# RWKV-7 recurrence and top-k expert layer on one core: 32 by 32 blocks to and from GpSimd's inversion, by transfers or by VectorE's turns

## The chip, the cores and the metric

The kernel runs on one core of one Trainium2 chip, whose engines are TensorE (PE), VectorE (DVE), ScalarE (ACT), GpSimd (POOL) and SyncE (SP). The metric is device time in microseconds (us) of one execution of the whole kernel, lower is better. Profiles show one execution; its span (first to last instruction) and its own time stand beside the median of the timed runs below.

## What is computed

The first part is a recurrence over 768 tokens for 4 batches of 8 heads with head size 40, each with a 40 by 40 state. The second part routes each of the 3072 output rows (320 wide) to one of 8 experts, keeps the 80 rows with the highest gate weight per expert, and runs them through a two-layer network:

```
for t in range(S):                       # S = 768
    y[t]  = r[t] @ state
    Sa    = state @ a[t]
    state = state * w[t] - outer(Sa, b[t]) + outer(v[t], k[t])

x = y as (3072, 320);  logits = x @ w_gate
expert = argmax(logits);  gate = softmax(logits)[expert]
per expert e: keep the 80 rows of largest gate
out[rows] = gate * (relu(x[rows] @ w1[e]) @ w2[e])   # other rows are zero
```

## The kernel before, in words

**Units.** The sequence is cut into 12 chunks of 64 tokens; the 4 batches go in 2 pairs. A unit is one chunk of one pair, 24 units in all, n = 2 * chunk + pair. In a unit all 8 heads of both batches are handled together; one "block" is the 64 by 64 triangular matrix of one head and batch, 16 blocks in a unit. Within a chunk the recurrence becomes matrix products, with one inverse of a 64 by 64 unit-triangular matrix for each block.

**`prepare(n)`** (L498) loads w, a, k, b, forms the running products of w (two scans on VectorE, L514 and L522), turns and scales, and makes the score matrices: `nt` (the matrix to be inverted) and `psi`. It holds `P`, `ah`, `kb`, `psi` of a unit in rings of LOOK = 9 (L262), so unit n can only be prepared once unit n - 9 is done with them; `nt` has a ring of 8 units, so unit n's scores also need unit n - 8 to be done with its inverse. **`finish(n)`** (L732) loads r and v, uses the inverse (L846, L865), adds up outputs and the new state (L901, L914, L934, L939), and hands the output rows to **`gate`** (L971), once for four units (for two units at the very end). A unit's finish needs the state of the unit two before.

**The inverse.** For the first four units it is made by repeated squaring on TensorE (`doubling`, L419). For units 4 to 23, in five batches of four units, it goes by halves: each 64 by 64 matrix has two 32 by 32 diagonal blocks, 128 of them in a batch, which GpSimd inverts, one block in each of its 128 partitions, by 60 row steps (L648, L650), an `affine_select` and a `memset` (L655). So 32 by 32 blocks that lie across 32 partitions have to be laid flat, one in each partition, and back. `invert` (L601) does this through three tensors in HBM:

- SyncE writes the blocks out (`out_go`, L623, four DMAs) and GpSimd fetches them flat into `lt` (L632); SyncE also clears the lower left corners of `nt` (L640);
- after the steps GpSimd makes a flat transposed copy `ltT` (`flip`, L661) and writes both out (L668);
- SyncE brings them back: `solved` into `d1` (L677, four DMAs) and into `nt` (L684), `flipped` into `d0` (L690).

**`solve(n)`** (L698) joins the halves of a unit: matmuls G (L708) give, with all 128 rows as contraction over block-diagonal operands `d0`, an off-diagonal product that ScalarE copies to `gt` (L713); matmuls X (L723) with `d1` give the corner, which ScalarE copies into `nt` (L728). One join is eight matmuls of 128 rows, 64 columns, 64 wide.

**Ranks.** `gate` keeps for each group of four units the 80 best of 128 new and 80 old gate values in a row: ten rounds of `max` (L1026) and `match_replace` (L1028) over 208 columns on VectorE, five groups (`ranks`, L1022). Then the rows are joined in 8 partitions (L1041 to L1050), and three sets of ten rounds over 320, 336 and 336 columns follow, the last when the last two units have their gates. From their result `best` the selection, the gather and the expert layer follow.

**What sets the order.** All instructions of the first part are given to `Plan` (L18) with a planned duration, a due time and the tiles they read and write. `Plan.order` simulates the engines and writes down one fixed order for each engine (PE, DVE, ACT, POOL, and SP for its DMAs); ring reuse and PSUM banks are dependencies in it. A table `WISH` (L148) shifts due times by kind of operation and stage, `SAME` and `SWITCH` price a change between whole-array and tiled matmuls. On the chip each engine works through its order and waits where a semaphore isn't there yet; an SP DMA that waits holds every later SP DMA. With `held_back` (L739) the loads of r and v of a unit also wait for its batch's blocks to have been written out.

**Second part.** When the first part's buffers are free, the weights of 8 experts (L1095 to L1098) stream in on SP's queue while the selection runs; then 6 passes of gather, two layers and scatter.

Of the kernel before, what the change touches and what calls it, by code (L numbers as in the profile page):

```python
# [17 lines left out]
class Plan:  # L18
# [7 lines left out]
    def add(self, eng, us, lag, when, fn, reads=(), writes=(), psum=None, to=()):  # L26
# [21 lines left out]
        self.ops.append(o)  # L48

# [95 lines left out]
SAME = 88.8  # L145
WHOLE = ("wT", "aT", "ivT", "kbTp", "rvT", "sTp", "xp", "gp", "G", "X")
USE_TAIL = True
WISH = {  # L148
    "ACT UL": (4.2, 0, 19.2), "ACT VL": (-96.9, 27.8, -94.1), "ACT W": (2.1, 0, -24.8),
    "ACT W0": (-34.4, -152.3, -9.7), "ACT d0": (0.7, 20.3, -15), "ACT d1": (-14.1, 5.1, 10.3),  # L150
    "ACT dec": (5.1, 3.5, -35.1), "ACT el": (0, -105.4, -111.1), "ACT gt": (-14.2, 9.3, 21.8),
    "ACT ivc": (0.6, 0, 22.4), "ACT kbT": (46.6, 4.9, 29.8), "ACT nt": (-170.6, -112.1, 3.6),
    "ACT rawa": (11.7, 40.7, -2.7), "ACT rawb": (6.6, 0, -61.5), "ACT rs": (-8.4, 69.6, 4.2),
    "ACT rv": (22, 7.8, 4.1), "ACT sT": (14.3, -12.2, -3.8), "ACT uT": (59.9, -9.9, -23.9),
    "ACT xg": (8.9, 22.7, 4.9), "DVE P": (167.3, -8.9, 23.5), "DVE UL": (9.8, -12.3, -5.5),
    "DVE VL": (-65.4, -31.3, 3.6), "DVE W": (-36.1, -44.8, -5.4), "DVE ah": (73.7, 4.7, -113.1),
    "DVE begins": (14.6, 5.3, 15.4), "DVE cd": (240.3, 350.6, -16.3), "DVE consts": (-2, -35.6, -2.3),
    "DVE d0": (86.6, 16.4, -85.6), "DVE d1": (0, -24.8, 9.6), "DVE dec": (-11, 63.1, 27.1),
    "DVE ends": (-16.2, -79.7, 10), "DVE gates": (-23.5, 11, -44.9), "DVE gsm": (22.7, -33.7, 18.8),
    "DVE iv": (-0.2, 1.7, -5.2), "DVE jn": (10.1, 207.1, 243.7), "DVE kb": (-48, 7.9, -240.3),  # L160
    "DVE late": (-46.4, 1.9, 2.3), "DVE lg": (68.6, -5, -39.1), "DVE lt": (6.9, 26.2, 0),
    "DVE ltT": (-2.7, -53.8, 0.6), "DVE nt": (6.3, 0, -12.2), "DVE psi": (52.4, 66, -77.2),
    "DVE rawa": (4.8, 17.7, -76.6), "DVE raww": (10.4, -32, -11.4), "DVE rs": (0, 8.3, -30),
# [16 lines left out]
}  # L180
RQ = "SP"
VQ = "SP"
ALPHA = 1.9451


@with_exitstack
def kernel(
# [29 lines left out]
    GU = 4  # L217
# [53 lines left out]
    with ExitStack() as p1:  # L271
# [24 lines left out]
        def group(name, n):  # L296
            return wide[name][(n // GU) % WIDE[name]]
# [4 lines left out]
        def bank(key):  # L302
            return plan.home[key]
# [115 lines left out]
        def doubling(n, z, kn):  # L419


            def spare(name):
                return quads_of(name, n)
# [873 lines left out]
```

## Time and profile before

| | |
|---|---|
| median of 3 runs | 583.64 us (580.11 to 585.15) |
| the profiled execution | 579.1 us |
| its span | 577.3 us |
| PE busy | 450.2 us (78%) |
| DVE busy | 342.2 us (59%) |
| ACT busy | 208.8 us (36%) |
| POOL busy | 222.1 us (38%) |
| mean granted TensorE clock | 0.907 |
| last copy of a recurrence output (L964) ends | 465.1 us |
| `best` complete | 479.6 us |
| first expert matmul (L1224) | 501.9 us |

Busy is time in which an engine ran an instruction. The five inversions on GpSimd work from 92.7 to 132.7, 175.2 to 216.9, 237.4 to 277.6, 305.5 to 345.9 and 371.1 to 407.8 us (first step to the memset). In the views, x counts instruction records: each fp32 matmul shows as two, so the eight matmuls of a join are "x16". "idle before" is what the engine stood still before an instruction, and behind the arrow what ended it; "issue" there means that the profile shows nothing that it waited for.

### The profile page before, as it was taken

What the parts mean: (1) busy time and instruction counts of PE and PEld (TensorE: products, weight loads), DVE (VectorE), ACT (ScalarE), POOL (GpSimd) and SP (SyncE); (2) the same over time, 40 slices, a digit from 0 to 9 for tenths busy, and PEclk for the clock granted to TensorE, in tenths of its full rate; (3) what the DMA queues carried; (4) which work ended last, traced back from release to release, by engine and by line L of the source; (5) the groups of instructions that cost most, each with busy time, mean ns of one, the idle gap of its engine ahead of it and who ended that gap; (6) DMA issues with size and microseconds to landing.
All of it is one profiled execution on the core that took longest, in us unless ns stands there. A gap on an engine that the chain in (4) does not pass through costs nothing. (4 is left out here: it accounts for less than half of the span.)

```text
span 577.3 us, 28139 instructions
## 1 busy us (share of the span) xinstructions
PE 450.2 (78%) x12655; PEld 370.3 (64%) x12655; DVE 342.2 (59%) x752; ACT 208.8 (36%) x424; POOL 222.1 (38%) x412
## 2 busy tenths in 40 slices
PE   3878977788688988389976998698759813399996
PEld 2767767778687977289876897588648712134432
DVE  8878863556357865486643675875478897112211
ACT  2435543545434654145524463344414300011010
POOL 7000005882107982588407982388400010400101
PEclk9989998989979998699979998799969965599999
DMA  8745572614987648845789335721530139999200
GB/s 137 120 70 94 95 134 61 102 49 99 262 143 149 99 91 202 168 71 112 158 148 182 59 82 133 156 37 33 139 84 16 26 99 359 348 344 342 86 13 17
DMA packets 243452, 73.91 MB, mean 128 GB/s; under 512 B 216484, under 2 KB 237988, under 8 KB 243332
## 3 DMA queue, kind: packets, MB, share of 16 engines
q1 hardware_dynamic: 218292, 51.15, 43.4%
q10 hardware_dynamic: 22304, 11.29, 7.3%
q0 software_dynamic: 2736, 9.67, 5.0%
q8 instruction: 99, 1.62, 1.2%
q14 instruction: 21, 0.17, 0.1%
HBM read 52.11 MB, written 16.72 MB: 119 GB/s over the span
## 5 line engine op out<-in xcount | busy, mean ns | idle before, releaser
L648 POOL TENSOR_TENSOR tmp<-lt 128x30 f32<-128x30 f32 (+9 forms) x150 | 82.9, 553 | 27.3 <-DMA lt<-blocks 15.9
L650 POOL TENSOR_TENSOR lt<-lt,tmp 128x30 f32<-128x30 f32 (+9 forms) x150 | 85.0, 567 | 11.7
L632 POOL DMA_DIRECT2D lt<-blocks x5 | 3.0, 596 | 142.9 <-PE ps L468 76.9
L575 PE MATMUL ps<-ah,kbT 40*64 40x64 f32 x1536 | 33.8, 223 | 9.8 <-issue 8.0
L575 PEld LDWEIGHTS ps<-ah,kbT 40*64 40x64 f32 x1536 | 28.1, 136 | 11.9 <-issue 7.8
L754 ACT COPY VL<-rawv 128x320 f32<-128x320 f32 x24 | 11.0, 459 | 64.5 <-PE ps L901 55.4
L901 PE MATMUL ps<-UL,kb 64*64 64x128 f32 x768 | 29.9, 291 | 4.8 <-DVE UL L789 3.2
L564 ACT COPY kbT<-ps 128x1024 f32<-128x1024 f32 x24 | 24.4, 1015 | 24.0 <-PE ps L408 21.1
L514 DVE TENSOR_TENSOR_SCAN P<-dec,begins 128x520 f32<-128x520 f32 x24 | 32.1, 1337 | 0.6
L522 DVE TENSOR_TENSOR_SCAN iv<-dec,ends 128x520 f32<-128x520 f32 x24 | 31.8, 1326 | 0.7
L1255 POOL DMA_INDIRECT out_dram<-y,idx_s x6 | 6.0, 997 | 66.8 <-DVE y L1254 66.8
L789 DVE TENSOR_TENSOR UL<-ps,mask 128x512 f32<-128x512 f32 x24 | 16.5, 689 | 25.1 <-PE ps L782 24.9
L901 PE MATMUL ps<-VL,kb 64*64 64x128 f32 x768 | 29.4, 288 | 0.7 <-issue 0.7
L408 PE MATMUL ps<-ident,kb 128*128 128x128 f32 x192 | 27.7, 290 | 2.1 <-DVE kb L547 1.1
L1224 PE MATMUL hp<-w,xe 128*32 128x512 f32 (+1 forms) x128 | 28.4, 643 | 0.7 <-DVE xe L1214 0.7
L1252 PE MATMUL yp<-w,hT 128*64 128x320 f32 (+1 forms) x256 | 28.6, 435 | 0.3 <-DVE hT L1243 0.3
L944 DVE TENSOR_TENSOR xT<-ps,P 128x512 f32<-128x512 f32 x24 | 16.5, 687 | 20.9 <-PE ps L901 20.9
L708 PE MATMUL ps<-d,nt 128*64 128x64 f32 x320 | 16.1, 250 | 15.6 <-issue 8.0
L765 ACT COPY rv<-ps 128x1024 f32<-128x1024 f32 x24 | 24.4, 1015 | 9.7 <-PE ps L408 9.7
L901 PEld LDWEIGHTS ps<-UL,kb 64*64 64x64 f32 x768 | 23.6, 143 | 6.6 <-DVE UL L789 4.0
L914 PE MATMUL ps<-rv,sT 40*64 40x64 f32 x768 | 23.8, 232 | 4.7 <-issue 4.7
L956 PE MATMUL ps<-wsel,xT 128*128 128x88 f32 x192 | 25.8, 279 | 0.8 <-DVE xT L944 0.8
(201 smaller groups left out, 1117.8 us busy)
## 6 DMA issues: line engine op xcount, KB each, us to landing
w<-in_moe_w_dram SPq DMA_DIRECT2D x8, 1280.0 KB, 14.3
w<-in_moe_w_dram SPq DMA_DIRECT2D x8, 1024.0 KB, 15.5
x_rows<-xg ACTq DMA_DIRECT2D x24, 160.5 KB, 3.8
rawk<-in_k_dram SPq DMA_DIRECT2D x48, 80.0 KB, 3.3
raww<-in_w_dram SPq DMA_DIRECT2D x48, 80.0 KB, 3.2
rawr<-in_r_dram SPq DMA_DIRECT2D x48, 80.0 KB, 3.0
rawv<-in_v_dram SPq DMA_DIRECT2D x48, 80.0 KB, 2.9
out_dram<-zero ACTq DMA_DIRECT2D x8, 480.0 KB, 3.3
```

Source lines behind the costliest of these rows:

```text
L408: nc.tensor.matmul(o, lhsT=i, rhs=ident, start=True, stop=True, is_transpose=True, skip_group_check=True)
L514: nc.vector.tensor_tensor_scan(at("P", n), at("dec", n)[:, 0 : H * SEG], begins, 0.0, op0=Alu.mult, op1=Alu.add)
L522: nc.vector.tensor_tensor_scan(at("iv", n)[:, H * SEG : 0 : -1], at("dec", n)[:, H * SEG : 0 : -1], at("ends", n)[:, H * SEG : 0 : -1], 0. ...
L564: nc.scalar.copy(at("kbT", n).rearrange("p (k c) -> p k c", k=2), ps[:, bank(kk) : bank(kk) + 2, :])
L575: nc.tensor.matmul(ps[T * o : T * o + T, b0 + q, T * i : T * i + T], lhsT=at("kbT", n)[rows, 512 * x + c : 512 * x + c + T], rhs=at("ah", ...
L648: e.tensor_tensor(out=tv, in0=t3[:, 0:s, s : s + 1].to_broadcast([np_, s, n]), in1=t3[:, s : s + 1, s + 1 :].to_broadcast([np_, s, n]), op ...
L650: e.tensor_tensor(out=t3[:, 0:s, s + 1 :], in0=t3[:, 0:s, s + 1 :], in1=tv, op=Alu.add)
L765: nc.scalar.copy(at("rv", n).rearrange("p (k c) -> p k c", k=2), ps[:, bank(kr) : bank(kr) + 2, :])
L901: nc.tensor.matmul(ps[HB * q : HB * q + HB, b0 + bb, 128 * i : 128 * i + 128], lhsT=at("kb", n)[rows, o : o + HB], rhs=view(at(name, n)[ro ...
L956: nc.tensor.matmul(ps[:, b0, o : o + 88], lhsT=at("xT", n)[:, 128 * i : 128 * i + 128], rhs=wsel[:, i, :], start=True, stop=True, skip_gro ...
L1224: nc.tensor.matmul(hp[j][c], lhsT=xe[:, i, c], rhs=weights[e][0][:, i, FH * j : FH * j + FH], start=i == 0, stop=False)
L1252: nc.tensor.matmul(yp[c], lhsT=hT[:, f, c], rhs=weights[e][2][:, f, :], start=f == 0, stop=f == FK - 1)
```

## The change

1. **Blocks by turns.** The three HBM tensors and all transfers of `invert` are gone. VectorE's `transpose`, which turns each 32 by 32 square within 32 partitions, moves the blocks: three turns in (one over all 128 partitions with 1024 columns, two over 32 partitions with 1024 columns, strided views), then the same GpSimd steps, then four turns out: `d0` and `tb` (128 partitions each) and two of 32 partitions back into `nt`. The flat copy `flip` and the corner clearing are gone; the copy of the scores into `nt` leaves the corner out (three ScalarE copies in place of one, the corner is zeroed once by GpSimd at the start).
2. **Joins on 32-row tiles.** `d0` and `tb` hold only 32 by 32 blocks. G and X are sixteen matmuls each: 32 rows, 32 or 64 columns, 32 wide, into two PSUM banks (before: one); `gt` and the corner are copied with two ScalarE copies of 32 or 64 partitions each. G and X are no longer listed as whole-array in the planner.
3. **Ten units in flight.** LOOK is 10; `P`, `ah`, `kb`, `psi` of a unit lie in one tile. Slots 8 and 9 serve first as scratch of the doubling in place of the old `d0` and `d1`; half of the doubling's `plus` lies in the new `d0`.
4. **Ranks of 16 units at once.** Groups 0 to 3 lay their 128 values side by side; ten rounds over 512 columns follow at group 3, ten over 208 columns at group 4. The later sets stay.
5. **Planner.** New `WISH`, `ALPHA`, `SAME`; planned durations for the new operations (1.2 us for a turn, 1.53 us for a round over 512). The r and v loads are no longer held back.

```diff
-    blocks, solved, flipped = (nc.dram_tensor(name, (len(batches), 2, 2, 2, GU * H // 2, C * C), F32, kind="Internal")
-                               for name in ("blocks", "solved", "flipped"))
-    LOOK = 9
+    LOOK = 10
...
             if n >= GU:
                 def nt_go():
-                    nc.scalar.copy(quads_of("nt", n), quads(kn).rearrange("p q (i t) -> p q i t", t=T))
+                    o, i = quads_of("nt", n), quads(kn).rearrange("p q (i t) -> p q i t", t=T)
+                    nc.scalar.copy(o[:, :, :, C:], i[:, :, :, C:])
+                    for x in range(2):
+                        rows = slice(T * x, T * x + C)
+                        nc.scalar.copy(o[rows, :, :, 0:C], i[rows, :, :, 0:C])
...
         def invert(kq):
+            def by_s(c):
+                return view(group("nt", ns[0]), C * c, (1, C), (T, C))
+            by_h = view(lt, 0, (1, C), (C, C))
+            for x, c in ((None, 0), (0, 1), (1, 1)):
+                rows = slice(0, 128) if x is None else slice(T * x + C, T * x + T)
+                add("DVE", 1.2, 0.1, z, lambda rows=rows, c=c: nc.vector.transpose(by_h[rows], by_s(c)[rows]),
+                    [("nt", n) for n in ns], [lk])
 ...
-            add("SP" if x == 0 or whole else "ACT", 0.8 * 2 * len(qs), 2.4, z, out_go, [("nt", n) for n in ns], [("blk", kq, x)])
-            add("POOL", 1.0, 4.6, z, fetch, [("blk", kq, 0), ("blk", kq, 1)], [lk])
-            add("SP", 0.7 * 2 * len(qs), 1.9, z, clear_go, (), [("nt", n) for n in ns])
...
-            add("POOL", 2.05, 0.1, z + 4.1, flip, [lk], [("ltT", kq)])
-            add("POOL", 1.0, 3.7, z + 4.2, put("lt", solved), [lk], [("sol", kq)])
-            add("POOL", 1.0, 4.6, z + 4.3, put("ltT", flipped), [("ltT", kq)], [("flp", kq)])
-            add("SP", 2.9, 2.0, z + 5, d1_go, [("sol", kq)], [("d1", n) for n in ns])
-            add("SP", 0.8 * 2 * len(qs), 2.6, z + 5, d0_go, [("flp", kq)], [("d0", n) for n in ns])
-            add("SP", 0.8 * 2 * len(qs), 3.2, z + 5, nt_back_go, [("sol", kq)], [("nt", n) for n in ns])
+            add("DVE", 1.2, 0.1, z + 5, lambda: nc.vector.transpose(view(at("d0", kq), 0, (1, C), (C, C)), lt.rearrange("p (s t) -> p s t", s=C)),
+                [lk], [("d0", kq)])
+            add("DVE", 1.2, 0.1, z + 5, lambda: nc.vector.transpose(view(at("tb", kq), 0, (1, C), (C, C)), by_h), [lk], [("tb", kq)])
+            for x in range(2):
+                rows = slice(T * x, T * x + C)
+                add("DVE", 1.2, 0.1, z + 5, lambda rows=rows: nc.vector.transpose(by_s(0)[rows], by_h[rows]), [lk], [("nt", n) for n in ns])
...
+            def joined_by(key, rows_of, lhs, rhs, outs):
+                b0 = bank(key)
+                for q in range(2):
+                    for i in range(M4):
+                        for x in range(2):
+                            rows = slice(*rows_of(x))
+                            o = C * (M4 * q + i)
+                            nc.tensor.matmul(ps[outs(x), b0 + x, o : o + C], lhsT=lhs(rows, q, i), rhs=rhs[rows, q, i, :],
+                                             start=True, stop=True, skip_group_check=True)
-            held_back = [("blk", batch_of[n], 1)] if n >= GU else ()
...
-                ranks(cd, nx, [("cd", gi), ("cd", gi + 1)], 0.89, False)
+                if lastly:
+                    ranks(later, nx, [("cd", 1), ("cd", 0)], 0.89, False)
+                elif len(groups[gi + 2]) < GU:
+                    ranks(early, later, [("cd", 0), ("cd", 1)], 1.53, False)
```

## The prediction

> **What bounds the kernel now.** I read the busy shares first, then stage sums, then the waits in order of time, and last the costs of single groups. The stage sums come from the table of windows, cut where joins of a batch begin (163, 240, 302, 365, 425 us), at the end of the recurrence (465) and before the expert layer (502). Columns: stretch and length, then busy us of PE, PEld, DVE, ACT, POOL.
>
> ```profile
> 163.00:240.00 77.00, 64.00 (x1834) 57.11 (x1826) 54.27 (x125) 35.24 (x72) 44.62 (x80) 0.92 0.69 138
> 240.00:302.00 62.00, 52.71 (x1608) 48.08 (x1609) 35.41 (x69) 25.65 (x53) 36.99 (x60) 0.89 0.66 125
> 302.00:365.00 63.00, 55.21 (x1733) 49.78 (x1733) 38.22 (x70) 30.73 (x64) 39.92 (x69) 0.97 0.57 114
> 365.00:425.00 60.00, 42.19 (x1394) 38.54 (x1394) 38.69 (x124) 20.50 (x47) 36.49 (x72) 0.86 0.46 99
> 425.00:465.00 40.00, 35.47 (x1187) 31.78 (x1187) 33.46 (x96) 14.09 (x35) 0.39 (x2) 0.95 0.08 16
> 465.00:502.00 37.00, 6.44 (x38) 4.11 (x40) 23.32 (x73) 1.14 (x7) 8.14 (x16) 0.52 0.87 283
> 502.00:577.30 75.30, 69.43 (x511) 29.05 (x511) 13.83 (x23) 7.85 (x20) 5.98 (x6) 0.95 0.52 169
> ```
>
> PE leads everywhere up to 425 us, but it is idle for 13.0, 9.3, 7.8 and 17.8 us there, 47.9 in all. From 417.5 (gates of group 4, timeline) to 479.6 (`best`) VectorE sets the pace: ranks, units 20 to 23 and gates follow one another. The timeline shows what PE stood still for:
>
> ```profile
> 243.50 1.12 PE L708 MATMUL ps<-d,nt 128*64 128x64 f32 x16 [7.60 <-issue]
> 371.35 1.09 PE L723 MATMUL ps<-d,gt 128*64 128x64 f32 x14 [4.83 <-DMA d<-solved]
> 425.29 1.33 PE L708 MATMUL ps<-d,nt 128*64 128x64 f32 x16 [6.86 <-DMA d<-flipped]
> ```
>
> All three are joins that wait for blocks. The first is named "issue", but its `d0` DMA was issued at 239.90, behind one of 8.22 us for `d1`. The steps had been over since 216.9, so the way back took 26.6 us; the last batch took 17.5 (407.8 to 425.3). The way in is 12 to 13 us (225.5 to 237.4, 292.8 to 305.5, 358.0 to 371.1). The steps themselves take 37 to 42 us.
>
> ```profile
> 407.65 0.16 POOL L658 MEMSET lt<- 128x32 f32 x1
> 408.10 0.60 POOL L668 DMA_DIRECT2D solved<-lt  x1 [0.30 <-POOL lt L658]
> 408.71 1.96 POOL L662 COPY ltT<-lt 128x1024 f32<-128x1024 f32 x1
> 410.97 0.53 POOL L668 DMA_DIRECT2D flipped<-ltT  x1 [0.30 <-POOL ltT L662]
> 415.06 2.24 SPq L677 DMA_DIRECT2D d<-solved  x4
> 417.35 1.09 SPq L684 DMA_DIRECT2D nt<-solved  x2
> 421.46 1.51 SPq L690 DMA_DIRECT2D d<-flipped  x2
> ```
>
> [...] no turn is in this trace. [...] the turns step by 256 and 128 bytes. [...] the strided reduce of 128x384 (L1156) took 1.096 us. [...] before joins I see gaps of 0.17 us at 436.24 and 439.18.
>
> **A turn.** TENSOR_TENSOR takes 689 ns for 512 columns (L789) and 485 for 320 (L833): 1.06 ns a column plus 145. For 1024 columns that is 1.23 us, if strides cost nothing. If they cost as in L1156, (1096 - 145) / 384 = 2.48 ns, it is 2.7 us; [...]. I take 1.23, which is near the planner's 1.2; its other VectorE durations (1.3 for a scan, 0.7 for a masked copy) agree with the rows (1.33, 0.69). Below 1.1 us no row gives a reason to go. 35 turns (7 in 5 batches) are 43 us.
>
> **Ranks.** The rows:
>
> ```profile
> L1026 DVE MAX8 cand<-cand 128x8 f32<-128x208 f32 x50 | 18.8, 375 | 1.3
> L1028 DVE MATCH_REPLACE8 cand<-cand,cand 128x208 f32<-128x208 f32 x50 | 17.9, 359 | 0.0
> ```
>
> With the 92 ns value load a round is 0.83 us, ten are 8.3, five sets 41.3. MAX8 over 336 takes 499 ns, so 0.97 ns a column and 0.67 us for 512; MATCH_REPLACE8 likewise 0.64. A wide round is 1.41, ten are 14.1; with group 4's 8.3 it is 22.4. That removes 18.9 us, all before 417 us, where VectorE has slack (38.7 of 60 us busy even in the stretch with most ranks). VectorE up to 465: 305.0 - 18.9 + 43 = 329 us. It costs and gives nothing directly; cover gone, it would be +24.
>
> **ScalarE.** The copy into `nt` goes from 0.586 to three of about 0.37 (the 256-column row L713), so +0.53; `gt` and the corner gain +0.37 each: 1.27 us times 20 units is 25 us, 200 to 225 of some 440. Hidden, except that the first join of a batch gets 0.75 us longer while PE waits: 5 times, about +4.
>
> **PE.** A join is 16 records in 0.69 us (43 ns each, two column tiles at a time). After: 32 records. Lower bound: 64-row tiles, four at a time, go at 0.69 / 32 = 21.5 ns, so no change. Upper bound: 43 ns each, +0.69 a join, +27.6 for 40. They use two tiles in turn but stream half as many columns; I take +0.15 a join, +6. [...]
>
> **Path of the blocks.** In: about 4 us (three turns behind at most one VectorE instruction) for 12 to 13. Out: 1.2 us to `d0`, 2 to 5 to all, for 17 to 27. No SP queue, so 70 SP DMAs (14 a batch) no longer stand among the loads, and nothing of GpSimd's queue waits for a fetch. A turn that waits for `nt` or for GpSimd's memset holds VectorE's later masked copies and state sums, and PE behind those; in the built order they stand where the previous batch's work is still running. The first batch gains little: its `d0` turn needs a buffer that the doubling of units 2 and 3 holds, and that released the old flip at 148.6.
>
> **What the order says.** In the built program 15 units are finished when the fourth batch's joins begin (16 before) and 11 at the third's (12 before). So joins no longer stand behind the whole previous batch. In both orders the last unit is prepared when unit 14 is finished or just before unit 15 is, since `nt`'s ring of 8 still holds; LOOK 10 moves little.
>
> **The sum, up to 417.5 us.** Half of the 47.9 us of idleness goes, -24 (12.4 of it the two waits above; the third lies after 417.5 where VectorE sets the end, and counts nothing). First stretch: the joins began at 169.2 with a gap of 3.24 us at 160.3; -5. Gaps inside groups of matmuls ("issue", 0.9 to 2.3 us, some 20 us up to 417) get fewer with fewer packets: the 70 DMAs of 64 or 128 KB in 128-byte rows are 61 thousand of the page's 243,452. I take -4, from 0 to -10. PE joins +6, ScalarE +4. Turns hold a masked copy for up to one turn, twice a batch; 10 times some 0.2 us reach PE, +2 (0 to +12). Sum -24 - 5 - 4 + 6 + 4 + 2 = -21; the more overlapped joins of batches 3 and 4 let units 16 to 19, which take 46 us (371 to 417) with PE idle 18, close up by some 4 more: -25. After 417.5 VectorE's chain is the same 62 us, and 465 to 577 is unchanged. Span 577.3 - 25 = 552; the execution adds 1.8: 554. The median shown is 583.64 against 579.1 for the profiled run, a factor 1.008: 558 us.
>
> **Rivals.**
> - *Turns are strided-slow* (2.5 us): VectorE 374 of about 455 us, and the three turns in and up to four out take 7.5 and 10 us. Speaks for it: L1156. Half of the gain stays: 571.
> - *The transfers were hidden anyway*: only the two named waits go, less PE and ScalarE: 12.4 - 10 = 2.4 us, 581. Against it: the 17.8 idle us of 365 to 425.
> - *32-row tiles cost 43 ns a record*: +21.6 over the above, 580.
> - *All idleness but 12 us goes and the joins cost nothing*: -45, 538.
> - *VectorE becomes the bound, slower.* [...] at the 0.91 busy share that it reached in 450 to 480 (27.2 of 30), the recurrence ends at 480, +15: 599 in the median. It decides from 3.9 us a turn, where 286 + 35 x 3.9 = 0.91 x 465.
> - That blocks would still travel is excluded: the built GpSimd queue holds no fetch or put.
>
> **Chances.** Forecast 0.42, slow turns 0.20, hidden 0.13, all gone 0.12, VectorE bound 0.08, slow tiles 0.05. One percent, about what a measurement can tell from no change, is 578 to 589: faster 0.76 (forecast, all gone, most of slow turns, a third of hidden), same 0.13, slower 0.11. The range 538 to 584 leaves out the VectorE-bound case and the ends of the others. The forecast's own range is 550 to 566.
>
> **What would show it.** Right: turns near 1.2 us, joins near 0.7 to 0.85, no PE wait over 4 us before a join, gates of group 4 near 392, `best` 62 us later. Wrong: turns above 2 us, PE waiting for VectorE's masked copies, or the end after group 4 longer than 62 us.

## The result and the profile after

The changed kernel took 603.46 us (median of 4, 601.60 to 613.66) beside 584.39 us for the kernel before on the same chip (4 runs, 580.11 to 587.51): 1.032 times as long, with an interval of 1.023 to 1.041. I had forecast 558 us. The profiled execution took 602.45 us with a span of 600.7, against 579.1 and 577.3. Times of one kernel spread by up to 4%, and the longer ones show the lower mean clock of TensorE (0.857 in 613.66 us, 0.884 in 601.60); ratios and intervals leave disturbed runs out, and are missing where too few were left.

The stage sums of the changed kernel come from its table of windows, cut in the same places: where joins of a batch begin, at the end of the recurrence, and before the expert layer. The columns are those of the table of before: busy us of PE, PEld, DVE, ACT, POOL, then the granted clock, the DMA share and GB/s.

```profile
0.00:165.00 165.00, 125.60 (x4406) 111.27 (x4406) 120.62 (x188) 79.03 (x149) 51.24 (x106) 0.98 0.49 85
165.00:229.00 64.00, 57.24 (x1765) 52.71 (x1767) 49.42 (x69) 32.58 (x73) 37.81 (x65) 0.90 0.43 78
229.00:295.00 66.00, 59.67 (x1708) 53.80 (x1703) 45.11 (x65) 34.99 (x77) 38.83 (x65) 0.86 0.44 83
295.00:363.00 68.00, 61.16 (x1757) 56.51 (x1758) 50.86 (x73) 32.60 (x73) 38.45 (x65) 0.85 0.31 64
363.00:424.00 61.00, 58.37 (x1784) 54.85 (x1786) 43.94 (x76) 26.84 (x62) 32.50 (x65) 0.80 0.22 40
424.00:477.00 53.00, 45.28 (x1355) 41.91 (x1344) 36.12 (x107) 17.83 (x46) 1.04 (x5) 0.81 0.14 30
477.00:524.00 47.00, 6.53 (x39) 4.29 (x40) 32.85 (x102) 1.51 (x7) 8.23 (x16) 0.52 0.62 209
```

PE idles less, as forecast: 6.8, 6.3, 6.8 and 2.6 us in the four stretches from 165 to 424. Yet its busy time rose and its clock fell, to 0.80 to 0.90 where it had been 0.86 to 0.97. The waits of 5 to 8 us before joins are gone but for one of 4.1 us (the row of L670 below). Group 4's gates end at 432.6 us (417.7 before), the last unit's xT at 475.9 (463.4), `best` at 501.4 (479.6), and the first expert matmul starts at 523.7 (501.9): +15, +12, +22 and +22.

The timeline shows the last batch's way out, where the kernel before had two puts and three fetches:

```profile
410.80 0.15 POOL L646 MEMSET lt<- 128x32 f32 x1
...
418.04 1.97 DVE L648 STREAM_TRANSPOSE d<-lt 128x1024 f32<-128x1024 f32 x1
...
419.85 4.41 DVE L653 STREAM_TRANSPOSE nt<-lt 32x1024 f32<-32x1024 f32 x2
...
422.56 0.69 PE L670 MATMUL ps<-d,nt 32*32 32x32 f32 x32
...
424.28 1.99 DVE L650 STREAM_TRANSPOSE tb<-lt 128x1024 f32<-128x1024 f32 x1
...
426.95 1.17 PE L922 MATMUL ps<-wsel,xT 128*128 128x88 f32 x8 [2.52 <-DVE xT L910]
```

The steps are over at 411.0, but the first turn stands behind other VectorE work until 418.0; the four turns then hold VectorE for 8.2 us, and at 426.95 PE has waited 2.5 us for an xT behind them.

In the batches between, the four turns out of one batch stand close to the three turns in of the next:

```profile
219.26 4.44 DVE L653 STREAM_TRANSPOSE nt<-lt 32x1024 f32<-32x1024 f32 x2
223.73 0.69 DVE L755 TENSOR_TENSOR UL<-ps,mask 128x512 f32<-128x512 f32 x1
224.34 1.93 DVE L648 STREAM_TRANSPOSE d<-lt 128x1024 f32<-128x1024 f32 x1
226.11 1.98 DVE L650 STREAM_TRANSPOSE tb<-lt 128x1024 f32<-128x1024 f32 x1
228.13 6.44 DVE L629 STREAM_TRANSPOSE lt<-nt 128x1024 f32<-128x1024 f32 x3
```

Seven turns and one masked copy fill these 15 us. From 286.7 to 301.7 and from 352.7 to 369.0 it is the same, with one operation between and with three. The turn to `d0`, which the first join waits for, comes third here.

The ranks cost what the rows of before had said, 0.69 + 0.68 us a wide round:

```profile
L992 DVE MAX8 later<-early 128x8 f32<-128x512 f32 x10 | 6.9, 690 | 0.2
L994 DVE MATCH_REPLACE8 early<-later,early 128x512 f32<-128x512 f32 x10 | 6.8, 676 | 0.0
```

Two rows did not come out as I had assumed. A turn takes 2.0 to 2.2 us (groups of VectorE, with shapes kept apart), so 35 of them take 74 us, not 43:

```profile
L653 DVE STREAM_TRANSPOSE nt<-lt 32x1024 f32<-32x1024 f32 x10 | 22.1, 2209 | 0.1
L629 DVE STREAM_TRANSPOSE lt<-nt 32x1024 f32<-32x1024 f32 x10 | 21.3, 2132 | 0.3
```

And the joins take 46.8 us of TensorE records, where I had 6 more than the 32.3 of before. First the groups of the kernel before, then of the changed one:

```profile
L723 PE MATMUL ps<-d,gt 128*64 128x64 f32 x320 | 16.2, 246 | 5.6 <-DMA d<-solved 4.8 <-ACT gt L713 0.5 <-issue 0.3
L708 PE MATMUL ps<-d,nt 128*64 128x64 f32 x320 | 16.1, 250 | 15.6 <-issue 8.0 <-DMA d<-flipped 6.9 <-DVE lg L990 0.7
```

```profile
L670 PE MATMUL ps<-tb,gt 32*64 32x32 f32 x640 | 29.6, 249 | 0.5 <-ACT gt L682 0.5
L670 PE MATMUL ps<-d,nt 32*32 32x32 f32 x640 | 17.2, 210 | 5.9 <-DVE slot L555 4.1 <-ACT rv L731 1.1 <-ACT dec L518 0.7
```

Half the columns a record, twice the records, and 15 us more in all (a matmul of the program leaves two records here; the expectations below say "matmuls" for records in the joins).

**Where TensorE's time went.** I added up, from the trace, PE's busy and idle time until the last unit's xT, and the time at a granted clock of 0.5. In both traces the record of that clock shows only 1.0 and 0.5, and its stretches at half last 3.4, 6.8, 10.2, 13.7, 17.1 or 20.5 us there. For before and after: busy 373.2 and 406.2 us (+33.0), idle 90.2 and 69.6 (-20.6), at half clock 64.9 and 102.4. PE was busy in 44.0 of the 64.9 us and in 97.8 of the 102.4.

The clock weighs on the joins too: at full clock a record of the new joins took 28.7 ns of PE's time (before: 44.0), at half 47.8 (67.5). Two estimates from these traces explain the growth. At full-clock prices the joins would have cost 36.7 us for 28.2, 8.6 more. And from the start of one record to the next of its group, the recurrence's products took 1.6 to 1.9 times as long at half clock (27.5 and 48.7 ns for the 64x128 ones with `VL`, L867), so that some 43% of the busy time at half clock is lost: 42 us of 97.8, beside 19 of 44.0 before, 23 more. Together that is 32 of the 33.0 us. A later profile of the changed kernel (the last experiment) has 398.3 us busy, 72.3 idle and 81.9 at half, 75.5 of them busy: +25.1 of busy time, and the same estimates give 22. Two profiles of one kernel thus differ by 20 us at half clock, and differences of that size between single profiles are not evidence. Over all runs, though, the mean clock is 0.857 to 0.890 in the changed kernel (8 runs) and 0.887 to 0.915 in the kernel before (the 23 runs beside the last experiment).

The table of 3 us windows around the last turns shows one such loss. Columns as above; the granted clock is the third number from the end.

```profile
424.00:427.00 3.00, 0.48 (x32) 0.37 (x21) 2.99 (x4) 0.76 (x3) 0.00 (x0) 1.00 0.48 80
427.00:430.00 3.00, 3.00 (x44) 2.78 (x48) 2.79 (x10) 0.52 (x3) 0.00 (x0) 0.64 0.02 5
430.00:433.00 3.00, 3.00 (x106) 2.86 (x110) 0.98 (x6) 1.28 (x4) 0.65 (x3) 0.50 0.00 0
433.00:436.00 3.00, 3.00 (x114) 2.88 (x108) 0.49 (x1) 1.74 (x4) 0.00 (x0) 0.50 0.25 56
436.00:439.00 3.00, 3.00 (x51) 2.71 (x53) 1.36 (x3) 0.73 (x2) 0.00 (x0) 0.50 0.65 174
439.00:442.00 3.00, 3.00 (x78) 2.83 (x72) 1.25 (x5) 0.00 (x0) 0.00 (x0) 0.58 0.01 3
```

PE stands still from 424.4 for 2.5 us while VectorE turns. Then it is busy without a gap, and still at half clock until 441. The same follows the turns of the three batches before: half clock from 236.7 to 253.8, from 294.7 to 315.2 and from 363.0 to 380.1. The stretch shown also holds the transposition that group 4's ranks wait for: they start 6.0 us after the gates (438.6), where it was 1.1 us before.

### The profile page after: what moved, and what is told of

It reads as the page before. It is cut to its first block, busy times and chain, and to the rows that moved or that the text cites. A ratio compares the mean times of both kernels' runs of the same rounds, so it can differ in the third digit from the quotient of the medians.

```text
span 600.7 us, 29295 instructions
## 1 busy us (share of the span) xinstructions
PE 484.4 (81%) x13295; PEld 403.7 (67%) x13295; DVE 392.9 (65%) x697; ACT 233.2 (39%) x504; POOL 214.1 (36%) x393
## 2 busy tenths in 40 slices
DMA packets 174607, 56.14 MB, mean 93 GB/s; under 512 B 153652, under 2 KB 171060, under 8 KB 174484
## 5 line engine op out<-in xcount | busy, mean ns | idle before, releaser
L583 PE MATMUL ps<-slot,kbT 40*64 40x64 f32 x1536 | 33.0, 222 | 7.9 <-issue 6.6
L867 PE MATMUL ps<-UL,slot 64*64 64x128 f32 x768 | 34.3, 321 | 6.1 <-DVE UL L755 4.6
L522 DVE TENSOR_TENSOR_SCAN slot<-dec,begins 128x520 f32<-128x520 f32 x24 | 32.3, 1344 | 6.3 <-ACT dec L518 5.8
L583 PEld LDWEIGHTS ps<-slot,kbT 40*64 40x64 f32 x1536 | 27.8, 134 | 11.2 <-issue 8.6
L867 PE MATMUL ps<-VL,slot 64*64 64x128 f32 x768 | 33.4, 312 | 0.2 <-issue 0.2
L867 PEld LDWEIGHTS ps<-UL,slot 64*64 64x64 f32 x768 | 26.8, 159 | 9.5 <-DVE UL L755 6.4
L922 PE MATMUL ps<-wsel,xT 128*128 128x88 f32 x192 | 28.2, 293 | 5.9 <-DVE xT L910 5.7
L629 DVE STREAM_TRANSPOSE lt<-nt 32x1024 f32<-32x1024 f32 (+1 forms) x15 | 32.1, 2137 | 0.3
L720 ACT COPY VL<-rawv 128x320 f32<-128x320 f32 x24 | 11.0, 459 | 51.9 <-PE ps L867 50.8
L572 ACT COPY kbT<-ps 128x1024 f32<-128x1024 f32 x24 | 24.4, 1015 | 17.1 <-PE ps L413 13.9
L670 PE MATMUL ps<-tb,gt 32*64 32x32 f32 x640 | 29.6, 249 | 0.5 <-ACT gt L682 0.5
L922 PEld LDWEIGHTS ps<-wsel,xT 128*128 128x128 f32 x192 | 25.0, 203 | 7.5 <-DVE xT L910 3.9
L670 PEld LDWEIGHTS ps<-tb,gt 32*64 32x64 f32 x640 | 27.1, 168 | 3.1 <-issue 1.0
## 6 DMA issues: line engine op xcount, KB each, us to landing
w<-in_moe_w_dram SPq DMA_DIRECT2D x8, 1280.0 KB, 14.5
```

Source lines behind the costliest of these rows:

```text
L522: nc.vector.tensor_tensor_scan(at("P", n), at("dec", n)[:, 0 : H * SEG], begins, 0.0, op0=Alu.mult, op1=Alu.add)
L572: nc.scalar.copy(at("kbT", n).rearrange("p (k c) -> p k c", k=2), ps[:, bank(kk) : bank(kk) + 2, :])
L583: nc.tensor.matmul(ps[T * o : T * o + T, b0 + q, T * i : T * i + T], lhsT=at("kbT", n)[rows, 512 * x + c : 512 * x + c + T], rhs=at("ah", ...
L629: add("DVE", 1.2, 0.1, z, lambda rows=rows, c=c: nc.vector.transpose(by_h[rows], by_s(c)[rows]), [("nt", n) for n in ns], [lk])
L670: nc.tensor.matmul(ps[outs(x), b0 + x, o : o + C], lhsT=lhs(rows, q, i), rhs=rhs[rows, q, i, :], start=True, stop=True, skip_group_check=True)
L867: nc.tensor.matmul(ps[HB * q : HB * q + HB, b0 + bb, 128 * i : 128 * i + 128], lhsT=at("kb", n)[rows, o : o + HB], rhs=view(at(name, n)[ro ...
```

## The experiments

All but two kernels keep the changed kernel's order of instructions, or that of the kernel before; where the planner made a new order, it is said. "Last unit" is the end of the last unit's xT in the profiled execution.

**1. What a turn costs by itself.** Put behind the emission of the plan, in a loop of two:

```
+            nc.vector.transpose(d0_, tb_)
+            nc.vector.transpose(d0_, view(tb_, 0, (1, C), (C, C)))
+            nc.vector.transpose(view(d0_, 0, (1, C), (C, C)), tb_)
+            nc.vector.transpose(d0_[:, 0:512], tb_[:, 0:512])
+            nc.vector.tensor_copy(d0_.rearrange("p (s t) -> p s t", s=C), tb_.rearrange("p (s t) -> p s t", s=C))
+            nc.vector.tensor_copy(d0_.rearrange("p (s t) -> p s t", s=C), tb_.rearrange("p (s t) -> p t s", s=C))
```

> The changed kernel with six extra VectorE operations, twice each, behind the last ranks: fp32 turns of 128x1024 with both sides contiguous, with the input alone strided by 128 bytes, with the output alone strided by 128 bytes, a contiguous turn of 512 columns, and copies of 1024 columns with a contiguous and with a 128-byte strided input. Theory 'strides cost': the contiguous turn takes 1.1 to 1.3 us (0.6 to 0.7 for 512 columns), one strided side 1.6 to 2.0, and the strided copy is slower than the contiguous one by as much. Rival [...] all three turns of 1024 columns take 1.9 to 2.2 us, 512 columns 1.0 to 1.1, and the two copies differ by under 10%.

The groups of VectorE; L1058, L1059 and L1060 are the first three rows of the edit:

```profile
L1060 DVE STREAM_TRANSPOSE d<-tb 128x1024 f32<-128x1024 f32 x2 | 3.8, 1910 | 0.1
L1059 DVE STREAM_TRANSPOSE d<-tb 128x1024 f32<-128x1024 f32 x2 | 3.8, 1900 | 0.1
L1058 DVE STREAM_TRANSPOSE d<-tb 128x1024 f32<-128x1024 f32 x2 | 2.5, 1230 | 0.0
```

A contiguous turn takes 1.230 us, what the prediction worked out; that it agrees to the nanosecond is luck, since 512 columns take 0.712 where the same formula gives 0.69. That is 1.01 ns a column. One strided side makes it 1.90, whichever side, and with both sides strided the kernel's own turns take 2.0 to 2.2. The copies took 0.693 and 1.032. "Strides cost" holds; a turn is not slow by itself.

**2. Turns twice.** Each `nc.vector.transpose(...)` of the five edits became `[nc.vector.transpose(...) for _ in range(2)]`.

> The changed kernel with each of the 35 turns issued twice in place, the order of all else unchanged: 74 us more of VectorE work. Theory 1 (the 31 us by which the turns are longer than planned are what the kernel lost): the time rises by 40 to 75 us, to 643 to 678. Rival (the turns lie beside other work, and the loss is on TensorE): up to 12 us more, 603 to 615. Theory 3 (the granted clock falls when TensorE is kept busier): where the time rises, TensorE idles more and the mean clock comes back from 0.87 to 0.89 or more.

677.45 us, 1.173 (1.166 to 1.180) of the kernel before: by the medians 74 us over the changed kernel's 603.46, by the ratios 82, for 74 us of turns, the upper end of theory 1. (The changed kernel's median comes from another chip; here and below the ratios, each to the kernel before on its own chip, compare better.) PE idles 134.4 us up to the last unit instead of 69.6. The third expectation fell the other way: the mean clock went down to 0.832, and 177.5 us ran at half. So the clock does not fall because PE is too busy.

**3. Turns halved.** The first of five edits; the others are alike, and `tb` is cleared once ahead. The kernel leaves out half of each block.

```
-lambda rows=rows, c=c: nc.vector.transpose(by_h[rows], by_s(c)[rows])
+lambda rows=rows, c=c: nc.vector.transpose(by_h[rows, 0:16], by_s(c)[rows, 0:16])
```

> The changed kernel with each turn over half of its columns (512 of 1024), so that half of each block keeps old values, and one memset ahead; order unchanged. A turn then takes about 1.05 us, 37 us less VectorE work, near the 1.23 us of the prediction. Theory 1 (the turns' duration is why the prediction failed): 560 to 575. Rival (it is TensorE's joins and clock, or the new order): 592 to 603, and with the prediction's own price of a turn paid the kernel is still not faster than before.

576.18 us (median of 12), 0.995 (0.991 to 0.998) of the kernel before. A turn took 1.08 to 1.19 us. The time lies just above theory 1's range and far below the rival's: 27 us less by the medians, 22 by the ratios, for 37 us less VectorE work. With the price that the prediction had for a turn, the kernel only ties with the one before; that part of the rival's words stands. In the profile, one of its longest executions (581.63 us), PE's idle time is 58.1 us (-32 against before), and 78.5 us run at half clock, which is no clear fall beside the 102.4 and 81.9 of the changed kernel.

**4. Joins twice.** `for q in range(2)` in `joined_by` became `for q in (0, 1, 0, 1)`.

> The changed kernel with every matmul of its joins issued twice (1,280 more records of 32x32), order unchanged. Theory 2 (the joins on 32-row tiles cost TensorE about 47 us and lie on the path): the time rises by 30 to 47 us, to 633 to 650. Rival (joins hide in TensorE's idle 70 us): up to 12 us more. Theory 3 (clock): with TensorE busier the mean clock falls below 0.865, and rows that the edit does not touch, the 64x128 matmuls of the joined products and states first of all, get longer than 0.32 us.

649.79 us, 1.122 (1.115 to 1.130): 46 us more by the medians, 52 by the ratios, for 45 us of records, theory 2's upper end. The mean clock fell to 0.846 and 150.2 us ran at half, though PE was busy for 456.9 of 523.5 us. Together with experiment 2 this changed theory 3: neither busy nor idle time alone goes with the clock. I cut the recurrences of the 18 profiles into steps of 3.4 us, the shortest stretch at half, and summed, over PE's records in each, columns times the used share of the array's rows and columns; a 32x32 record counts with a sixteenth of its columns. Of 349 steps at half clock with PE over 97% busy, 192 were followed by another at half; their sum was some 900 on the average, against some 1,660 where the clock came back. In the profile of the changed kernel these are 14 of 23 steps, in that of the kernel before none of 7. Theory 3 in its new form takes from this correlation that the small joins, and not waits alone, keep the changed kernel at half clock.

**5. Full-array matmuls behind the joins.**

```
+                for _ in range(4):
+                    nc.tensor.matmul(ps[:, b0, 256:384], lhsT=ident, rhs=ident, start=True, stop=True, skip_group_check=True)
```

> The changed kernel with four extra full-array matmuls (128x128 by 128 columns, fp32, of the identity with itself, into unused columns of the join's own PSUM bank) behind each of the 40 joins; order unchanged. 160 matmuls of about 0.2 us are 34 us more TensorE work. Theory 3 in its new form ([...] 102 us of the recurrence run at half in the changed kernel, 65 in the kernel before): the half-rate time of the recurrence falls under 70 us, the 64x128 matmuls get shorter than 0.31 us, and the time rises by less than 20 us. Rival (any 34 us of TensorE work on the path cost 34 us, as the doubled joins cost 46): the time rises by 30 to 40 us and the half-rate time stays near 100.

611.57 us, 1.058 (1.049 to 1.068); 8 us over the changed kernel by the medians, 15 by the ratios. The half-clock time fell to 47.8 us and the mean clock rose from 0.873 to 0.920 (0.907 to 0.931 in the four runs). The joined products, which the edit does not touch, got shorter; the changed kernel's row, then this one's:

```profile
L867 PE MATMUL ps<-UL,slot 64*64 64x128 f32 x768 | 34.3, 321 | 6.1 <-DVE UL L755 4.6 <-issue 1.4
```

```profile
L869 PE MATMUL ps<-UL,slot 64*64 64x128 f32 x768 | 28.9, 293 | 5.3 <-DVE UL L757 5.3
```

And so did the joins themselves, 40.2 us for the same 1,280 records that took 46.8:

```profile
L670 PE MATMUL ps<-tb,gt 32*64 32x32 f32 x640 | 24.1, 223 | 0.7 <-ACT gt L684 0.5
L670 PE MATMUL ps<-d,nt 32*32 32x32 f32 x640 | 16.1, 201 | 8.4 <-DVE slot L555 4.6 <-DVE d L648 1.4 <-ACT sT L857 0.9
```

PE's busy time grew by only 17 us (406.2 to 423.0; by 25 against the second profile), though the added records hold PE for 50.7. The three expectations of theory 3 came in (47.8 us at half, 293 ns, 8 to 15 us more); but the filling costs more than the clock returns.

**6. The same behind the joins of the kernel before** (order of the kernel before).

> The kernel before with four full-array matmuls behind each of its 40 joins, 160 in all and 34 us of TensorE work; order unchanged. Theory 3: its joins use all 128 rows [...] so the filling saves less than in the changed kernel: half-rate time 40 to 60, time 595 to 610. Rival (the full-array matmuls help any kernel with 64-row products as they helped the changed one, +8): 580 to 590.

610.44 us, 1.051 (1.045 to 1.057), PE's busy time +42 us (373.2 to 415.0), half-clock time 64.8 us as without the edit. So there 160 full matmuls cost 0.26 us each and gave nothing back; the half-clock time, which I had expected to fall a little, did not move. Beside experiment 5 (+17 to 25 us of busy time for the same work, half-clock time down to 47.8) this speaks for the small joins, and not waits alone, keeping the changed kernel's clock down.

**7. Ranks of before; wide ranks over one group only; the plan with longer turns.** Three attempts on the order and the end.

> The changed kernel with the ranks of before: ten rounds over 208 columns for each group instead of ten over 512 for four groups at once; the planner orders it anew with the same wishes. 19 us more VectorE work, but 14 us less of it stands directly ahead of group 4's ranks. Theory 4 (the wide ranks come late, group 4's ranks wait for them, and the end after the last unit grew by 9 us): from the last unit's xT to the end of the span it goes back from 125 to about 115 us, and the time is 590 to 598. Rival (VectorE's work as such counts, at 0.7 to 1 us per us): 610 to 625.

603.42 us, 1.043 (1.033 to 1.052); from the last unit to the end 122.1 us instead of 124.9 (113.9 before). Neither theory: 19 us more of VectorE work cost nothing that stands out, and the end did not come back.

> The changed kernel with the ten wide rounds over one group's 128 columns instead of all 512, so that the thresholds come from a part of the candidates; order unchanged, 9 to 10 us less VectorE work, all between 390 and 416 us. Theory 4 (wide ranks hold units 16 to 19 and group 4's ranks): 593 to 598. Rival (VectorE has room there): 600 to 605.

Here `part = src[:, 0:128]` took the place of `src` in the wide rounds, so that three groups are left out: 599.30 us, 1.039 (1.029 to 1.049), no measurable gain.

> The changed kernel with the planner booking 2.2 us for each turn in place of 1.2, nothing else: the same instructions in another order. Theory 5 (the order was made for turns of 1.2 us and is wrong for those of 2.1): 588 to 597. Rival (the turns' work itself, not its placing, sets the time): 599 to 610.

605.63 to 622.21 us in four runs, median 620.13, no ratio. No run shows a gain; whether this order is worse isn't shown. The later edits keep the old one.

**8. Fewer turns, work given to ScalarE.**

```
                         nc.scalar.copy(o[rows, :, :, 0:C], i[rows, :, :, 0:C])
+                        nc.scalar.copy(o[low, :, :, 0:C], i[low, :, :, C:])
...
+                    if x is None:
+                        nc.vector.transpose(by_h, by_s(0))
+                    else:
+                        nc.scalar.copy(group("nt", ns[0])[rows].rearrange("p (h t) -> p h t", t=T)[:, :, 0:C],
+                                       zero[rows, :, 0:1].to_broadcast([C, C, C]))
...
                 nc.vector.transpose(view(tb, 0, (1, C), (C, C)), by_h)
+                for x in range(2):
+                    rows = slice(T * x, T * x + C)
+                    nc.scalar.copy(group("nt", ns[0])[rows].rearrange("p (h t) -> p h t", t=T)[:, :, 0:C],
+                                   tb[rows].rearrange("p (h t) -> p h t", t=C))
...
-                add("DVE", 1.2, 0.1, z + 5, lambda rows=rows: nc.vector.transpose(by_s(0)[rows], by_h[rows]),
+                add("DVE", 1.2, 0.1, z + 5, lambda: None,
```

> The changed kernel with three turns a batch in place of seven and the whole output computed: ScalarE copies the lower corners into columns 0 to 31 of their own rows as well, so that one turn of 128 rows brings all corners in, ScalarE then puts the zeros back, and ScalarE copies the solved upper corners from tb into nt instead of two turns; order unchanged. 44 us less VectorE work (20 turns of 2.1 to 2.2 us), some 25 us more on ScalarE. Theory 1 (turns on the path, slope 0.7 as in the halved turns): 568 to 578, near the halved turns' 576, with half-rate time in the recurrence under 85 us. Rival (ScalarE's copies take the turns' place on the path, two of over 1 us ahead of the joined products): 585 to 600.

610.86 us, 1.056 (1.050 to 1.062), and 105.8 us at half clock: with 44 us less on VectorE nothing was gained, and theory 1 in its plain form ("VectorE's time is what is lost") fell. The waits of PE and ScalarE's group show what came instead:

```profile
PE ps L761 <- ACT rv L744: 5.7, 4, 3.4
...
PE ps L683 <- ACT gt L695: 4.6, 2, 3.3
```

```profile
L661 ACT COPY nt<-tb 32x1024 f32<-32x1024 f32 x10 | 10.4, 1042 | 5.2 <-DVE tb L658 5.1
```

The copies of 1.04 us stand in ScalarE's queue ahead of `rv` and `gt`, and two of them wait for the turn into `tb` there. With two full-array matmuls behind each join:

> The same with two full-array matmuls (128x128 by 128 columns) behind each join, 80 in all and 17 us of TensorE work. Theory 3 [...]: half-rate time falls under 50 us, the mean clock is over 0.92, and the time is 560 to 573, not above that of the kernel without them. Rival (work on TensorE's path costs its length): 10 to 17 us more than without them.

619.11 us (median of 6, 604.94 to 623.01), no ratio, and 95.6 us at half clock. This expectation failed: with two full matmuls a join the time at half clock falls by 10 us at most, within what two profiles of one kernel differ by, the mean clock of the profile is 0.883, and the time is not under that without them. So this run doesn't show that the small joins hold the clock down.

**9. The same moves on GpSimd.** Memsets of the zeros and copies from `tb` went to `nc.gpsimd`, behind the inversion, where it would only wait.

> The kernel with three turns a batch, but with the zeros put back and the solved upper corners copied by GpSimd, behind its inversion, instead of by ScalarE; order unchanged, the whole output computed. If ScalarE's 1.04 us copies were what ate the gain of fewer turns, 575 to 590. If it was the two more copies of each unit's corner that stay on ScalarE (0.73 us a unit, ahead of the turn in) or a turn's own 2 us, 598 to 612.

581.69 us (median of 20, kernel before 581.52), ratio 0.992 (0.987 to 0.997): 29 us less than with the copies on ScalarE, the same 15 turns in both. So ScalarE's copies had eaten the gain. The ratio rests on 4 of the 20 runs; by the medians this is a tie with the kernel before. At last, ScalarE's part shortened (`nc.scalar.copy(o, i)` and the two lower corners, three copies for five):

> The kernel with three turns a batch and GpSimd's copies, and one copy of all 512 columns of a unit into nt on ScalarE (about 0.6 us) with the two lower corners behind it, in place of five copies (1.83 us): 0.5 us less a unit ahead of the turn in. If those copies still hold the pipeline, 3 to 8 us less than with five (581.7), so 573 to 579 and under the kernel before; rival (hidden): 579 to 584, no difference that can be measured to the kernel before.

578.44 us (median of 23, kernel before 581.71), 0.990 (0.987 to 0.993), a ratio that rests on 13 of the 23 runs; the medians of all give 0.994. It is at most 1% faster than the kernel before, and some 4% faster than the changed one. That the shorter copies on ScalarE brought the 3 us isn't shown, as the two kernels' runs overlap.

**10. Joins with half the records, and both costs at once.** The second kernel also has the halved turns of experiment 3, and leaves out what they leave out; in both, every second head gets its neighbour's correction.

```
-                    for i in range(M4):
+                    for i in range(0, M4, 2):
-                            nc.tensor.matmul(ps[outs(x), b0 + x, o : o + C], ..., rhs=rhs[rows, q, i, :],
+                            nc.tensor.matmul(ps[outs(x), b0 + x, o : o + 2 * C], ..., rhs=rhs[rows, q, i : i + 2, :],
```

> The changed kernel with 16 matmuls of 64 columns a join instead of 32 of 32 (each block of weights serves two heads, so every second head's correction is computed from its neighbour's block); the streamed columns and the order are unchanged, the count of records is that of the kernel before. Theory 2 (the joins' 14.5 us of extra TensorE time lie on the path, with what they do to the clock): 580 to 592, 12 to 22 us under the changed kernel on the same chip. Rival (the joins hide, and the slope of the doubled joins was only that of work added to a full engine): under 5 us less.

> The changed kernel with both: each turn over half of its columns, and 16 matmuls a join. Both costs are then about what the prediction gave them (turn 1.1 to 1.2 us, joins near those of before). If turn, joins and the clock that they pull down are the whole cause up to the last unit, the last unit is done at 440 us or before (475.9 in the changed kernel, 454.7 with half turns) and the time is 555 to 567; the 11 us that the end after the last unit grew by stay. Rival (something else, the new order or ten units in flight, holds the kernel up): 570 or more.

> The changed kernel once more, unaltered, as the reference on the same chip for the runs beside it: 598 to 610, 1.02 to 1.05 of the kernel before.

The changed kernel on this chip: 600.28 us, 1.031 (1.021 to 1.041). With half the joins' records: 588.34, 1.011 (1.003 to 1.020), 12 us less by the medians, 11 by the ratios, at the edge of theory 2's 12 to 22. With both: 559.93 us (median of 4, 550.03 to 572.17, no ratio), span 551.3, last unit at 425.8. One line of each table of windows, from 165 us to the last unit, for the kernel before, the changed kernel, and both costs taken down:

```profile
165.00:463.40 298.40, 246.46 (x7712) 222.65 (x7710) 198.25 (x477) 125.52 (x268) 158.41 (x281) 0.92 0.54 107
```

```profile
165.00:475.90 310.90, 280.65 (x8334) 258.82 (x8334) 224.42 (x383) 144.83 (x328) 148.63 (x265) 0.85 0.32 61
```

```profile
165.00:425.80 260.80, 241.29 (x7672) 218.69 (x7670) 197.64 (x380) 143.66 (x326) 149.80 (x265) 0.95 0.37 72
```

PE's busy time is back at that of the kernel before (241 for 246 us), its idle time falls from 51.9 us through 30.3 to 19.5, and the clock is at 0.95; 41.0 us of the recurrence run at half, against 64.9 and 102.4. The expected end at 440 us or before was reached with 14 us to spare. What was expected to stay stayed: from the last unit to the end of the span it is 125.4 us, as in the changed kernel (124.9), where it was 113.9 before. There VectorE's chain from group 4's gates to `best` sets the pace, and an earlier last unit doesn't shorten it by more than 2 us (60.0 for 61.9).

Up to the last unit, from the profiles:

| kernel | last unit, us | PE busy | PE idle | at half clock | group 4's gates to `best` |
|---|---|---|---|---|---|
| before | 463.4 | 373.2 | 90.2 | 64.9 | 61.9 |
| after | 475.9 | 406.2 | 69.6 | 102.4 | 68.8 |
| after, second profile | 470.6 | 398.3 | 72.3 | 81.9 | 65.6 |
| turns twice | 547.2 | 412.9 | 134.4 | 177.5 | |
| joins twice | 523.5 | 456.9 | 66.7 | 150.2 | |
| half turns | 454.7 | 396.6 | 58.1 | 78.5 | 66.6 |
| half joins | 457.8 | 384.7 | 73.0 | 71.7 | 63.2 |
| both halves | 425.8 | 371.5 | 54.3 | 41.0 | 60.0 |

By the medians, half turns give 24 us against the changed kernel's 600.28, half joins 12, and both 40 (the four runs of both spread over 22 us). The profiles say 16.3, 13.0 and 44.9 us of span against 596.2, but that of half turns is a long execution and that of both a short one. Whether the two gains do more than add up isn't shown. The clock would fit it: 78.5 and 71.7 us at half with one of them, 41.0 with both.

## Why the prediction was wrong

*The steps that failed are the price of a turn (1.23 us, measured 2.0 to 2.2), the step that hid the turns behind VectorE's slack (+2 us, where halving them gave 22 to 27), and the clock, for which the sum had no term; the joins' +6 us came to 14.5, most of the excess by the clock.* With the turns and records halved, the profiled execution has group 4's gates at 391.4 us (predicted 392), 60.0 us from there to `best` (62) and a span of 551.3 (552). That it meets the sum within 1 us is in part luck. Its four runs lie between 550.03 and 572.17 us, and it is one of the short ones. Its joins cost 30.3 us, 2 less than before, where the sum has 6 more; with that the sum would be 544. And PE is busy at half clock for 39.6 us, near the 44.0 of before, so that the missing term is small there. The prediction's own signs of being wrong all came in the changed kernel: turns above 2 us, PE waiting for VectorE (2.5 us for xT in the last batch), and 68.8 us instead of 62 after group 4.

- **A turn, 1.23 us.** Right for contiguous sides, and "if strides cost nothing" was the condition that failed: 2.0 to 2.2 us. The row that the prediction itself put up against it, the strided reduce, had pointed the right way, and its value of 2.5 was the nearer one. But it was no measure of a stride: a copy of 1024 columns lost 0.34 us by its strided side, a turn 0.67. The rival built on it, 571 us, was right on the duration and wrong on the consequence.
- **"VectorE has slack, so turns hide" (+2 us, 0 to +12).** This was the larger error. Taking away 37 us of turns gave 22 to 27 us, adding 74 cost 74 to 82. VectorE's average share says nothing here: four to seven turns stand together for 8 to 16 us and hold the masked copies and state sums; PE runs dry and, in the stretches named above, then runs at half clock. It is not a bound by VectorE's load, as that rival had it, deciding from 3.9 us a turn: at 2.1 us and a share of 0.73 of VectorE up to the last unit (345.0 of 475.9 us), the loss was there. And ScalarE's copies in place of turns cost as much as the turns, while on GpSimd they cost 29 us less (experiments 8 and 9): for the same moves the queue decided.
- **The way of the blocks.** Predicted 4 us in, 1.2 us out to `d0` and 2 to 5 us to all. In: the three turns alone take 6.4 to 7.4 us. Out: in the last batch 7.1 us pass between the steps' end and the first turn, then 8.2 us of turns; in the four last batches `d0` is there 9 to 11 us after the steps. It is shorter than by transfers (17.5 to the last batch's first join, now 11.6), but not by as much as forecast.
- **Half of PE's idleness goes.** Right in kind: with half turns it fell by 32 us, where the sum had 24 + 5 + 4 + 4 less 6 for turns and ScalarE; in the changed kernel the turns gave a third of that back (-20.6). Of the gaps, for which the sum had 4: PE's idle time that ended in "issue", up to group 4's gates, is 40.3 us before (7.6 of them a join's wait for blocks) and 20.5 after, and the DMA packets are 243,452 and 174,607; that the one brought the other isn't shown.
- **PE joins, +6 us (0 to +27.6).** 14.5 us in records; 11 to 12 us of time came back with half of the records. The price is inside the range. At full clock a record took 28.7 ns, near the 26 that +6 us means; at half clock 47.8, and 37 on the average. So the value was nearly right for the clock that it silently assumed.
- **The clock, no term.** By the estimate above some 23 us of PE's busy time, the joins' share included. The kernel before already ran 64.9 us at half, 44.0 of them with PE busy, and the sum left that out. Nor does a busy PE alone settle the clock: 192 of the 349 steps at half with PE over 97% busy were followed by another (experiment 4).
- **VectorE's chain of 62 us after group 4.** 68.8 us. 5 of the 7 us are the later transposition, which stood in PE's queue among joins at half clock; with both halves the chain is 60.0. That the wide ranks were the cause isn't borne out: old and narrow ranks moved the time by less than can be told.
- **Ranks, ScalarE's copies, first batch.** A wide round 1.46 us with its value load (1.41 predicted), a 32-row copy 0.36 us (0.37); the removal of 19 us of ranks gave nothing to be seen, as said.

What stays open: how much of the loss falls to the new order as such. With both costs down and the same order the predicted time is about reached (median 559.93 us), which leaves it little room, but no run gave the changed instructions the order of the kernel before. How the loss divides between turns and clock is an estimate: no run changed the clock and nothing else. The kernel at 0.990 still runs 32-row joins; one with fewer records and the whole computation wasn't tried.

## What to carry to other kernels

Price an operation in the layout it will have: a turn of 1.23 us with both sides contiguous took 2.0 to 2.2 with strides in the kernel. Where engines hand small pieces to each other, ask of each new operation what stands behind it in its queue and how long TensorE can live without that, not how busy the engine is on the average. And count TensorE's loss at the half clock too: here PE stood still for 2.5 us and then ran at half for 13.7 (427.8 to 441.5), busy nearly throughout, and at half clock the recurrence's products took 1.6 to 1.9 times as long.

## What the hardware did that I had not expected

- A busy TensorE did not always get its full clock back: in the 18 profiles 192 of 349 steps at half clock with PE over 97% busy were followed by another, and those had used less of the array (a sum of some 900 against some 1,660). This is a correlation over these traces, and the experiments on it differ: with full matmuls behind the joins the half-clock time fell from 102.4 us (in a second profile 81.9) to 47.8 in experiment 5, only from 105.8 to 95.6 in experiment 8, and not in the kernel before (64.9 and 64.8).
- An fp32 turn of 128x1024 took 55% longer with one strided side (1.90 us for 1.23), and up to 0.3 us more again with both; turns of 32 and of 128 partitions took 2.13 and 2.15 us for 1024 columns (L629).
- A join's record with 32 rows and 32 columns to stream was cheaper than one with 128 rows and 64 columns, but not by half: 28.7 against 44.0 ns of PE's time at full clock. On the average over the recurrence it is 37 against 50 (46.8 us over 1,280 records, 32.3 over 640), since more of the small ones run at half clock (520 of the 1,280, before 142 of the 640).
- A copy of 32x1024 took 1.04 us on ScalarE and 1.03 on GpSimd; twenty such moves, half of them zeros, made 29 us of difference in the kernel's time by the queue in which they stand.
